# Linformer attention and a two-layer feed-forward network on one core: reciprocals of block 4 and q of batch 3 ahead of batch 3's projections in the queue

## The chip, the cores and the metric

The kernel runs on one core of a Trainium2 chip. The metric is the device time of one execution in microseconds (us); smaller is better. Before the change the median of three runs was 490.59 us.

A core has a matrix engine (TensorE, "PE" in the profile; its weight loads are "PEld"), a vector engine (VectorE, "DVE"), an engine for activation functions and copies (ScalarE, "ACT"), a general engine (GpSimd, "POOL") and a sync engine ("SP") that here only issues transfers. Each engine runs its own program in order. All transfers, from whatever engine they are issued, run on the core's 16 DMA engines. Those issued by GpSimd form the "software" queue of the profile (q0), those issued by sync the "hardware" queue (q1).

## The reference: what is computed

Linformer attention, then a feed-forward network with a sigmoid-approximated GELU:

```python
# q, k, v: (8 batches, 8 heads, 1024, 64); E, F: (64, 1024)
k_proj = np.einsum('ks,bhsd->bhkd', E, k)
v_proj = np.einsum('ks,bhsd->bhkd', F, v)
scale = 1.0 / np.sqrt(q.shape[-1])
scores = scale * np.matmul(q, k_proj.transpose(0, 1, 3, 2))
scores = scores - np.max(scores, axis=-1, keepdims=True)
attn = np.exp(scores)
attn = attn / (np.sum(attn, axis=-1, keepdims=True) + 1e-09)
attn_out = np.matmul(attn, v_proj)
# ... then with x = attn_out as (8192 tokens, 512):
h = x @ w_in                                  # (512, 2048)
g = h * (1.0 / (1.0 + np.exp(-1.702 * h)))
out = g @ w_out                               # (2048, 512)
```

## The kernel before

The 8192 tokens are worked off in 16 blocks of 512; batch b has blocks 2b and 2b+1. The heavy products of a block are those of the network (steps `u*.P*` for the first layer, `F*` for the second). The attention of later blocks is woven between them. The order of everything from block 2 on is written down as a list of words, `STEPS`; in round `j` a word `name+d` does the step `name` for block `j + d`. The words that this text speaks of:

- `pj`: the projections k' and v' of a batch, from the loaded k and v. `kb`: a cast of k' by VectorE. `kd`: a transposing transfer that makes `kt` of it. `vq`: copies of v'.
- `ld`: loads of k and v of the batch after. `hold`: a tiny GpSimd copy that reads `kt`, so that GpSimd's next load waits for `kt`.
- `qd`: a transposing transfer that makes `qT` of the loaded q of a batch, and, in the kernel before, right behind it in the program the loads of q of the batch after.
- `sc`: scores of a block, from `qT` and `kt`. `ex`: their exponentials. `su`, `den`: their sums. `ga`: a transfer that spreads the sums over 128 partitions (the gather). `rc`: the reciprocals, by VectorE. `sr`: a transfer that writes them to DRAM (`rdr`). `sb`: two transfers that read them back, spread over 64 partitions each (`rbc`, the broadcast).
- `va`: the unnormalised attention output. `mv`: its product with `rbc`, by VectorE, which gives the input `xT` of the network.

```python
        elif i == "va":
            eight([new(f"V{t}{e}", [P, TB]) for e in range(2)], [vqs[b % 2][:, 2 * t + e, :] for e in range(2)],
                  [expT[j][:, 2 * t + e, :] for e in range(2)])
        elif i == "mv":
            u = 2 * int(p[1]) + t
            nc.vector.tensor_tensor(x_of(j)[:, u, :], live[f"V{p[1]}{t}"], rbc[j][:, u, :], op=ALU.mult)   # L713
        # ...
        elif i == "ga":
            gather(j)()                                                   # sync: rc <- den (block 4: rc <- o_sb)
        elif i == "rc":
            nc.vector.reciprocal(rdens[j], rdens[j])                      # L728
        elif i == "sr":
            n = rdens[j].shape[1]
            rdr[j] = dram.tile([HP, 2, TB], F32, name="rdr")
            nc.sync.dma_start(out=rdr[j].rearrange("p e (r n) -> (p e r) n", n=n), in_=rdens.pop(j))   # L732
        elif i == "sb":
            rbc[j] = att.tile([P, HP, TB], F32, name="rbc", bufs=1)
            for e, r in enumerate((LO, HI)):
                nc.sync.dma_start(out=rbc[j][r], in_=rdr[j][None, :, e, :].to_broadcast([D, HP, TB]))  # L736
        elif i == "pj":
            kvps[b] = new("PJ", [P, H, D])
            proj(b)()
        elif i == "hold":
            nc.gpsimd.tensor_copy(held, kts[b % 2][:1, 0, :1])            # L741
        elif i == "ld" and b + 1 < B:
            load_kv(k, kt, b + 1, "k_sb")
            load_kv(v, vt, b + 1, "v_sb")
        # ...
        elif i == "kd":
            nc.sync.dma_start_transpose(out=kts[b % 2], in_=tmps["kb"].rearrange("k h d -> k (h d)"))  # L749
        # ...
        elif i == "qd":
            q_dma(b)()
            if b + 1 < B:
                load_q(b + 1)
```

The bank numbers that matter: `F1.0` goes into bank 0, which `va` (V01) uses too; `pj` goes into bank 1, which the products `u1.*` and `u3.*` use too (A1):

```python
    BANK = dict(FD=0, FB=4, FG=0, A0=6, A1=1, B0=7, B1=3, G0=2, G1=5, S10=5, S11=7, V00=4, V01=0,
                S00=3, S01=2, V10=6, V11=5, D0=2, D1=5, PJ=1)
```

Round 2 differs from the later ones: the attention of blocks 4 and 5 and the projections of batch 3 are put in at places of their own, by a table of words `name@block` that are done right after a named word of the list:

```python
    AHEAD = {
        (2, None): "... va.0@3:6,1 va.1@3:5,7 mv.0.0@3 ... su@4:0,3 den.0@4 den.1@4 ga@4 ",
        (2, "u1.c1+1"): "F7.1@2",
        (2, "gs4.0"): "pj@6:1 kb@6 kd@6 vq.0@6 vq.1@6 hold@6 ld@6",
        (2, "F4.1"): "rc@4 sr@4 sb@4 qd@6",
    }
```

Of the kernel before, what the change touches and what calls it, by code (L numbers as in the profile page):

```python
# [17 lines left out]
def kernel(ctx, tc, q, k, v, E, F,  # L18
                                                     moe_w_in, moe_w_out, out):
    nc = tc.nc  # L20
    B, H, S, D = q.shape
# [495 lines left out]
    def ffn2_parts(j, d, e, f, last):  # L517
# [73 lines left out]
        ex.1.1+3 xs.2+1 gs3.1 F2.0 F2.1 ex.1.0+3 xs.1+1 kd+4 ex.0.1+3 F6.0 F6.1 Fc2 u0.c1+1 su+3 u1.c1+1 gt+1  # L591
        u0.P6+1 den.0+3 u0.P2+1 Fo0 den.1+3 gs4.1 u1.P6+1 F7.0 u1.P2+1 u1.P5+1 u0.c2+1 F5.0 u1.c2+1 u0.g11+1
        u1.c3+1 F5.1 ga+3 Fc3 u1.P7+1 F7.1 u1.g11+1 xs.3+1 gs4.0 u1.P3+1 u2.P1+1 u0.P5+1 u1.d1+1 u3.P1+1 Fd1
        u0.c3+1 u1.P4+1 F4.0 u0.P7+1 sb+2 u1.d2+1 u0.d1+1 qd+4 u1.g21+1 u3.c1+1 F4.1 u1.g12+1 u3.P6+1 u3.c2+1
        u0.P4+1 u1.g22+1 u3.P5+1 u0.P3+1 u0.g21+1
    """.split()
    BANK = dict(FD=0, FB=4, FG=0, A0=6, A1=1, B0=7, B1=3, G0=2, G1=5, S10=5, S11=7, V00=4, V01=0,
                S00=3, S01=2, V10=6, V11=5, D0=2, D1=5, PJ=1)
# [5 lines left out]
    def step(name, j, banks=None):  # L604
# [7 lines left out]
        i, t = p[0], int(p[-1]) if p[-1].isdigit() else p[-1]  # L612
# [17 lines left out]
        if i[0] == "F" and i[1:].isdigit():  # L630
            i = int(i[1:])
            n = ("FD", "FB", "FG")[OF[i]]
            if i in (1, 5) and t == 0:
                new(n, [P, 2, MH])
            x, w = ffn2_ops(j)[i]
            for c in range(FH):
                nc.tensor.matmul(live[n][:, t], x[:, c, t * P:(t + 1) * P], w[:, c],  # L637
                                 start=(i in (1, 5) and t == 0 and c == 0),
                                 stop=(i in (2, 3, 4) and t == 1 and c == FH - 1), skip_group_check=True)
        elif i == "Fc1":  # L640
            copy(new("FB", [P, 2, MH]), live["FD"])
        elif i in ("Fc2", "Fc3"):
            tmps[i] = work.tile([P, 2, MH], F32, name="u1_sb" if i == "Fc2" else "u2_sb", bufs=1)
            copy(tmps[i], live["FB" if i == "Fc2" else "FG"])
        elif i == "Fo0":
            nc.scalar.copy(o(0)[:, :, :MH], live["FD"])
        elif i == "Fo1":
            nc.scalar.copy(o(1)[:, :, :MH], live["FB"])
        elif i == "Fd1":
            add(o(1)[:, :, MH:], live["FB"], tmps["Fc3"])  # L650
        elif i == "Fd2":
            add(o(0)[:, :, MH:], live["FG"], tmps["Fc2"])
        elif i[:2] == "st":
            g = int(i[2])
            ov = out[b * S:(b + 1) * S, :].rearrange("(p j) m -> p j m", j=J)[:, c * JB:(c + 1) * JB]
            nc.sync.dma_start(out=ov[:, 2 * g:2 * g + 2], in_=outs.pop((j, g)))
        elif i[0] == "u":
            n, m = int(i[1]), int(i[1]) % 2
            if not uu:
                uu.append(ldpool.tile([P, 4, 2, TH], F32, name="q_even"))  # L660
            gts[j] = gT
            u1, u2 = uu[0][:, m], uu[0][:, 2 + m]
            lo, hi = slice(2 * n, 2 * n + 2), slice(FH + 2 * n, FH + 2 * n + 2)
            if t[0] == "P":
                i = int(t[1])
                x = xT[j]
                a, w = {
                    1: (a11, x[:, KLO, TLO]), 2: (a12, x[:, KHI, TLO]), 3: (late[:, 3], x[:, KHI, THI]),
                    4: (a22, xw[:, 3]), 5: (late[:, 0], xw[:, 0]), 6: (late[:, 1], xw[:, 1]),
                    7: (late[:, 2], xw[:, 2])}[i]  # L670
                h = "ABG"[OF[i]] + str(m)
                if i in (1, 5):
                    new(h, [P, 2, TH])
                for r in range(2):
                    for c in range(KC // 2):
                        f = (2 * n + r) * P
                        nc.tensor.matmul(live[h][:, r], a[:, c, f:f + P], w[:, c],  # L677
                                         start=(i in (1, 5) and r == 0 and c == 0),
                                         stop=(i in (2, 3, 4) and r == 1 and c == KC // 2 - 1), skip_group_check=True)
            elif t == "c1":  # L680
                nc.scalar.copy(new(f"B{m}", [P, 2, TH]), live[f"A{m}"])  # L681
            elif t == "c2":
                copy(u1, live[f"B{m}"], f"c2.{n}")
            elif t == "c3":
                copy(u2, live[f"G{m}"], f"c3.{n}")
            elif t == "d1":
                add(u2, live[f"B{m}"], u2)
            elif t == "d2":
                add(u1, live[f"G{m}"], u1)
            else:  # L690
                out_, in_ = {"g11": (gT[:, lo, TLO], live[f"A{m}"]), "g21": (gT[:, hi, TLO], live[f"B{m}"]),
                             "g22": (gT[:, hi, THI], u2), "g12": (gT[:, lo, THI], u1)}[t]
                nc.scalar.activation(out_, in_, AF.Gelu_apprx_sigmoid)  # L693
        elif i[:2] == "gs":
            g_sum(j, int(i[2]), 4 * t, 4)
        elif i == "xs":
            x_sum(j, t)
        elif i == "sc":
            if j not in expT:
                expT[j] = att.tile([P, HP, TB], BF16, name="expT", bufs=3)  # L700
            eight([new(f"S{t}{e}", [P, TB]) for e in range(2)], [kts[b % 2][:, 2 * t + e, :] for e in range(2)],
                  [qT[b][:, c * JB:(c + 1) * JB, 2 * t + e, :] for e in range(2)])
        elif i == "ex":
            u = int(p[1])
            nc.scalar.activation(expT[j][:, 2 * u + t, :], live[f"S{u}{t}"], AF.Exp, scale=scale)
        elif i == "gt":
            gelu_table()
# [6 lines that stand above are left out]
        elif i == "su":  # L714
            d_ps = [new(f"D{e}", [P, TB]) for e in range(2)]
            for q_ in range(HP):
                for e in range(2):
                    r = HI if (q_ + e) % 2 else LO
                    nc.tensor.matmul(d_ps[e][32 * q_:32 * q_ + 32], ones[r, :32], expT[j][r, q_, :], start=True, stop=True)  # L719
        elif i == "den":  # L720
            if j not in rdens:
                pool, n = (work, "o1_sb") if j == 4 else (att, "den")
                rdens[j] = pool.tile([P, 2, TB], F32, name=n, bufs=1)
            nc.vector.tensor_copy(rdens[j][:, t, :], live[f"D{t}"])
        elif i == "ga":
            gather(j)()
# [18 lines that stand above are left out]
        elif i == "kb":  # L745
            tmps["kb"] = att.tile([KP, H, D], BF16, name="k_b")
            copy(tmps["kb"], kvps[b][LO])
        elif i == "kd":
            nc.sync.dma_start_transpose(out=kts[b % 2], in_=tmps["kb"].rearrange("k h d -> k (h d)"))  # L749
        elif i == "vq":  # L750
            r, xs_ = ((LO, X_LO), (HI, X_HI))[t]
            copy(vqs[b % 2][r].rearrange("k (u e) d -> k u e d", e=2),
                 kvps[b][HI].rearrange("k (u x) d -> k u x d", x=4)[:, :, xs_, :])
        elif i == "qd":
            q_dma(b)()
            if b + 1 < B:
                load_q(b + 1)
        elif i != "ld":
            raise KeyError(name)

    FIRST = {"u": 3, "gs": 3, "xs": 3, "gt": 3, "va": 4, "mv": 4, "sc": 6, "ex": 6, "su": 5, "den": 5, "ga": 5, "rc": 5,
             "sr": 5, "sb": 5}
    BATCH = ("qd", "pj", "kb", "kd", "vq", "ld")

    def due(name, j, now):

# [78 lines left out]
    for j in range(NBLK):  # L845
# [34 lines left out]
    }  # L880

    def ahead(j, after):
# [54 lines left out]
```

The softmax here doesn't subtract the row's maximum and nothing guards it: scores larger than these inputs give would overflow.

## Time and profile before

| what | value |
|---|---|
| time, median of 3 runs | 490.59 us (488.91 to 491.72) |
| span of the profiled execution | 487.4 us |
| mean granted TensorE clock in it | 0.989 |
| busy share: VectorE, ScalarE, GpSimd | 65%, 66%, 17% |
| software queue q0: packets, MB | 86816, 30.43 |
| hardware queue q1: packets, MB | 46020, 37.84 |

How to read the profile: "busy" is the time in which an engine works on an instruction. A page cuts the span into 40 equal slices and gives the busy share of each as one digit (9 is 90% or more); a row `PEclk` gives the clock that TensorE was granted, in tenths. A line of waits such as `A x L1 <- B y L2: 10.1, 1, 10.1` says that engine A, ahead of its instruction at line 1 that writes x, sat idle 10.1 us, once, until B's y was there. The chain of waits follows the program from its end back, at each step to what released the instruction. Lines of the timeline have start, length, engine, line, operation, names (written `out<-in`) and count; a `q` behind an engine's name is its sequencer, which for transfers shows the issue, not the transfer. "Landing" is when a transfer's completion is seen.

### The profile page before, as it was taken

The numbers are of one execution on the slowest core, as the hardware profiler recorded it, in microseconds if no ns is written. First come the engines' busy times: TensorE is split into PE (matmuls) and PEld (weight loads), VectorE is DVE, ScalarE is ACT, GpSimd is POOL, SyncE is SP. The second block draws the span as 40 slices with busy tenths as digits, with TensorE's granted clock in tenths as the row PEclk, the third lists the DMA queues.
The fourth block names the chain that finished last, engine by engine and source line by source line (L and its number), as shares of the span: only waits on it lengthen the run. The fifth ranks groups of instructions, "written<-read, shape, count | busy, mean of one in ns | idle before, by whom it ended". The sixth has DMA issues, their size and how long they took to land.

```text
span 487.4 us, 10497 instructions
## 1 busy us (share of the span) xinstructions
PE 467.6 (96%) x4331; PEld 358.0 (73%) x4331; DVE 316.3 (65%) x587; ACT 322.3 (66%) x559; POOL 83.2 (17%) x104
## 2 busy tenths in 40 slices
PE   8999999998919999999999999999999999999997
PEld 4644457456817878787887878787887878888886
DVE  4503785596607585866858585866758586858562
ACT  2665466474617686867879686867878695849472
POOL 7562160151105010410105010500000000000000
PEclk9999999999978999999999999999999999999999
DMA  9999999899599569992999369992191423412022
GB/s 169 200 189 208 220 176 176 190 208 143 90 221 208 99 144 209 210 142 89 161 235 131 89 153 211 214 128 89 31 201 40 89 89 89 146 31 87 0 87 87
DMA packets 132963, 69.19 MB, mean 142 GB/s; under 512 B 98340, under 2 KB 122420, under 8 KB 132916
## 3 DMA queue, kind: packets, MB, share of 16 engines
q0 software_dynamic: 86816, 30.43, 54.7%
q1 hardware_dynamic: 46020, 37.84, 31.1%
q8 instruction: 34, 0.56, 0.5%
q10 hardware_dynamic: 80, 0.26, 0.2%
q14 instruction: 13, 0.11, 0.1%
HBM read 72.88 MB, written 16.99 MB: 184 GB/s over the span
## 4 chain that ended last, share of the span: by engine, by line
PE 87%; DMA 5%; ACT 3%; DVE 2%; issue 1%; POOL 1%; SPq 0%; DVEq 0%; ACTq 0%; POOLq 0%
PE k_ps L637 32%; PE k_ps L677 31%; PE k_ps L426 9%; PE k_ps L533 4%; PE k_ps L273 3%; PE k_ps L438 3%; PE k_ps L183 3%; DMA rbc<-rdr 2%; DMA q_even<-in_q_dram 2%; DMA rdr<-rc 1%; ACT gT L693 1%; PE k_ps L719 1%; DVE xT L713 1%; POOL k_sb L58 0%; PE k_ps L398 0%
## 5 line engine op out<-in xcount | busy, mean ns | idle before, releaser
L623 DVE TENSOR_TENSOR q_even<-k_ps,q_even 128x512 f32<-128x512 f32 x104 | 70.5, 688 | 54.4 <-PE k_ps L677 53.3
L677 PE MATMUL k_ps<-xw,late 128*128 128x256 bf16 x624 | 89.5, 273 | 0.6 <-DVE xw L499 0.6
L677 PEld LDWEIGHTS <-late 128*128 128x128 bf16 x832 | 80.4, 98 | 12.8 <-PE k_ps L637 2.3
L637 PEld LDWEIGHTS <-sg 128*128 128x128 bf16 x832 | 81.2, 98 | 10.7 <-issue 1.4
L693 ACT ACTIVATE gT<-k_ps 128x512 bf16<-128x512 f32 x104 | 62.3, 600 | 25.7 <-PE k_ps L677 24.1
L637 PE MATMUL k_ps<-tw,sg 128*128 128x256 bf16 x624 | 76.8, 273 | 0.3 <-DVE u_sb L620 0.3
L637 PEld LDWEIGHTS <-gT 128*128 128x128 bf16 x624 | 61.8, 99 | 18.8 <-issue 10.7
L677 PEld LDWEIGHTS <-w_in_sb 128*128 128x128 bf16 x624 | 58.5, 98 | 17.6 <-issue 10.9
L693 ACT ACTIVATE gT<-q_even 128x512 bf16<-128x512 f32 x104 | 61.6, 631 | 10.8 <-DVE q_even L623 10.8
L620 ACT COPY q_even<-k_ps 128x512 f32<-128x512 f32 x65 | 37.0, 591 | 42.8 <-PE k_ps L677 42.8
L637 PE MATMUL k_ps<-w_out_sb,gT 128*128 128x256 bf16 x416 | 53.3, 278 | 10.3 <-DVE xT L713 10.1
L677 PE MATMUL k_ps<-xT,w_in_sb 128*128 128x256 bf16 x416 | 62.3, 274 | 0.1
L70 POOL DMA_DIRECT2D q_sb<-in_q_dram x48 | 42.1, 905 | 114.3 <-DMA qT<-q_sb 89.2
L426 PE MATMUL k_ps<-xT,w_in_sb 128*128 128x512 bf16 (+1 forms) x200 | 42.7, 371 | 0.0
L507 DVE TENSOR_TENSOR sg<-gT 128x1024 bf16<-128x1024 bf16 (+2 forms) x64 | 41.4, 648 | 1.9 <-ACT gT L693 1.5
L428 ACT ACTIVATE gT<-k_ps 128x512 bf16<-128x512 f32 (+1 forms) x50 | 28.9, 580 | 18.0 <-PE k_ps L426 17.7
L713 DVE TENSOR_TENSOR xT<-k_ps,rbc 128x512 bf16<-128x512 f32 x52 | 33.4, 679 | 11.3 <-DMA rbc<-rdr 11.3
L426 PEld LDWEIGHTS <-w_in_sb 128*128 128x128 bf16 x200 | 19.3, 98 | 21.3 <-issue 0.8
L677 PE MATMUL k_ps<-xw,w_in_sb 128*128 128x256 bf16 x208 | 31.8, 276 | 0.0
L677 PE MATMUL k_ps<-xT,late 128*128 128x256 bf16 x208 | 31.2, 273 | 0.0
L681 ACT COPY k_ps<-k_ps 128x512 f32<-128x512 f32 x52 | 29.2, 587 | 2.7 <-DVE xT L713 1.2
L620 DVE COPY q_even<-k_ps 128x512 f32<-128x512 f32 x39 | 25.6, 683 | 8.1 <-PE k_ps L677 8.1
(136 smaller groups left out, 563.5 us busy)
## 6 DMA issues: line engine op xcount, KB each, us to landing
out_dram<-o_sb SPq DMA_DIRECT2D x31, 512.0 KB
rbc<-rdr SPq DMA_DIRECT2D x24, 512.0 KB
k_sb<-in_k_dram POOLq DMA_DIRECT2D x7, 1024.0 KB, 9.8
v_sb<-in_v_dram POOLq DMA_DIRECT2D x7, 1024.0 KB, 15.7
q_sb<-in_q_dram POOLq DMA_DIRECT2D x48, 128.0 KB, 6.2
w_in_sb<-in_moe_w_in_dram POOLq DMA_DIRECT2D x8, 256.0 KB, 10.3
w_out_sb<-in_moe_w_out_dram POOLq DMA_DIRECT2D x4, 512.0 KB, 11.5
q_even<-in_q_dram POOLq DMA_DIRECT2D x12, 128.0 KB, 12.9
```

Source lines behind the costliest of these rows:

```text
L70: nc.gpsimd.dma_start(out=qt[b][:, j], in_=qv[:, j])
L426: nc.tensor.matmul(h_ps, w_in_sb[:, kc, fc * P:(fc + 1) * P], xT[j][:, kc, ts], start=(kc == 0), stop=(kc == KC - 1))
L428: nc.scalar.activation(gts[j][:, fc, ts], h_ps, AF.Gelu_apprx_sigmoid)
L507: nc.vector.tensor_tensor(t[i - 1], in0, in1, op=ALU.add if i == 1 else ALU.subtract)
L533: nc.tensor.matmul(dst, a[:, k, tc_ * P:(tc_ + 1) * P], w[:, k], start=(first and (one or tc_ == 0) and k == 0), stop=(final and k == FH - 1),
L620: (nc.scalar.copy if n in ON_ACT else nc.vector.tensor_copy)(out_, in_)
L623: nc.vector.tensor_tensor(out_, in0, in1, op=ALU.add)
L637: nc.tensor.matmul(live[n][:, t], x[:, c, t * P:(t + 1) * P], w[:, c], start=(i in (1, 5) and t == 0 and c == 0), stop=(i in (2, 3, 4) and ...
L677: nc.tensor.matmul(live[h][:, r], a[:, c, f:f + P], w[:, c], start=(i in (1, 5) and r == 0 and c == 0), stop=(i in (2, 3, 4) and r == 1 an ...
L681: nc.scalar.copy(new(f"B{m}", [P, 2, TH]), live[f"A{m}"])
L693: nc.scalar.activation(out_, in_, AF.Gelu_apprx_sigmoid)
L713: nc.vector.tensor_tensor(x_of(j)[:, u, :], live[f"V{p[1]}{t}"], rbc[j][:, u, :], op=ALU.mult)
```

## The change

Two groups of words of round 2 become one, at one place: behind `u2.P1+1`, which lies two words behind `gs4.0` (where the projections stood) and ahead of `F4.1` (where the reciprocals stood). In the new group the reciprocals of block 4, their write and broadcast and the transpose of q of batch 3 come ahead of the projections of batch 3. The loads of q of the batch after are taken out of `qd` into a word of their own, `lq`, so that they can stand elsewhere than behind `qd`: in round 2 they are the last of the group, behind the k and v loads of batch 4, which still wait for `kt`. In the later rounds `lq` follows `qd` at once. No computation is added or left out.

What it is for: on the sync queue the write and the broadcast of the reciprocals are issued ahead of the transposes of q and k', and ahead of batch 4's loads on GpSimd's queue, rather than behind those loads.

```diff
@@ STEPS @@
-        u0.c3+1 u1.P4+1 F4.0 u0.P7+1 sb+2 u1.d2+1 u0.d1+1 qd+4 u1.g21+1 u3.c1+1 F4.1 u1.g12+1 u3.P6+1 u3.c2+1
-        u0.P4+1 u1.g22+1 u3.P5+1 u0.P3+1 u0.g21+1
+        u0.c3+1 u1.P4+1 F4.0 u0.P7+1 sb+2 u1.d2+1 u0.d1+1 qd+4 lq+4 u1.g21+1 u3.c1+1 F4.1 u1.g12+1 u3.P6+1
+        u3.c2+1 u0.P4+1 u1.g22+1 u3.P5+1 u0.P3+1 u0.g21+1
@@ step @@
         elif i == "qd":
             q_dma(b)()
-            if b + 1 < B:
-                load_q(b + 1)
-        elif i != "ld":
+        elif i == "lq" and b + 1 < B:
+            load_q(b + 1)
+        elif i not in ("ld", "lq"):
             raise KeyError(name)
@@ AHEAD @@
-        (2, "gs4.0"): "pj@6:1 kb@6 kd@6 vq.0@6 vq.1@6 hold@6 ld@6",
-        (2, "F4.1"): "rc@4 sr@4 sb@4 qd@6",
+        (2, "u2.P1+1"): "rc@4 sr@4 sb@4 qd@6 pj@6:1 kb@6 kd@6 vq.0@6 vq.1@6 hold@6 ld@6 lq@6",
```

The words between the two places, in the list:

```python
# gs4.0 u1.P3+1 u2.P1+1 u0.P5+1 u1.d1+1 u3.P1+1 Fd1 u0.c3+1 u1.P4+1 F4.0 u0.P7+1 ... F4.1
```

More of the change, by code (lines that the diff above doesn't have):

```diff
@@ L762 @@
              "sr": 5, "sb": 5}
-    BATCH = ("qd", "pj", "kb", "kd", "vq", "ld")
+    BATCH = ("qd", "pj", "kb", "kd", "vq", "ld", "lq")
     def due(name, j, now):
```

## The prediction

> **What bounds the kernel now.** I read the engine totals first, then the slices, then the waits of the one slice that stands out, then the chain through it, then the queues that feed it. By the totals TensorE is busy 467.6 us, 96% of the span, VectorE 65%, ScalarE 66%. Two rows of the 40 slices (12.2 us each):
>
> ```profile
> PE   8999999998919999999999999999999999999997
> ...
> PEclk9999999999978999999999999999999999999999
> ```
>
> TensorE is full nearly everywhere, so an instruction that it is spared, or a wait that it is spared, moves the end one to one. There is one hole: the slice with the 1 (134 to 146 us), followed by slices with a lower granted clock. After it every slice is 9 until the last. The waits between 112 and 160 us (engine, line waited for, total us, times, longest):
>
> ```profile
> DVE xT L713 <- DMA rbc<-rdr: 11.3, 1, 11.3
> ...
> PE k_ps L637 <- DVE xT L713: 10.1, 1, 10.1
> ```
>
> VectorE's normalisation of block 4 (`mv`, L713) waits for rbc, the broadcast reciprocals; TensorE waits for VectorE because the next product F1.0 goes into the bank that `mv` has to read first. The chain of waits through the hole (start, us, what):
>
> ```profile
> 127.72 6.43 DMA rdr<-rc
> ...
> 134.96 10.10 DMA rbc<-rdr
> ```
>
> The reciprocal (0.27) ends right ahead of the first line, and `mv` starts at 145.19, 0.1 us after the last. So 17 us of transfers (16 KB out, then 2 x 512 KB back) stand between the reciprocal and `mv`. Why so slow? The sync queue, and GpSimd's, in order of time:
>
> ```profile
> 114.51 0.57 SPq L322 DMA_DIRECT2D rc<-o_sb  x1
> 116.71 0.52 SPq L322 DMA_DIRECT2D rc<-den  x1
> 123.49 1.18 SPq L749 DMA_TRANSPOSE kt<-k_b  x1
> 127.72 0.34 SPq L732 DMA_DIRECT2D rdr<-rc  x1
> 134.23 1.34 SPq L736 DMA_DIRECT2D rbc<-rdr  x2
> 135.89 10.57 SPq L263 DMA_TRANSPOSE qT<-q_sb  x1
> ```
>
> ```profile
> 126.31 0.87 POOL L58 DMA_DIRECT2D k_sb<-in_k_dram  x1 [0.31 <-issue]
> 127.17 0.88 POOL L58 DMA_DIRECT2D v_sb<-in_v_dram  x1
> ```
>
> The k and v loads of batch 4 went out 1.4 and 0.6 us ahead of the 16 KB write, and everything after them crawls. Before they went out the engines had nothing to do. DMA from 118 to 128 us, in slices of 0.25 us:
>
> ```profile
> GB/s 154 155 164 157 145 109 93 62 28 30 33 13 0 0 0 0 0 0 0 0 0 0 0 33 0 0 36 165 61 1 0 0 0 0 0 0 0 0 0 29
> ```
>
> The gather of block 4 (`rc<-o_sb`, issued 114.51; `rc<-den` is that of block 5) sat among the q loads of batch 3. In the single packets, its 128 pieces are read by 119.6, those of block 5 by 121.0, where this row falls to 0. So the sums of block 4 lie there at about 120, and until 127.7 the row shows next to nothing but the small kt transpose: the reciprocals could have been taken and sent.
>
> [...] 16 KB took 6.43 us behind the loads, and 1.7 us from issue to landing for the rdr write that GpSimd issued at 94.04. [...] in the single DMA packets no rbc packet appears until about 4 us after its issue at 134.23, then both queues run. [...] The trace has exactly one such drop: granted clock 0.50 from 142 to 150 us, 0.88 from 150 to 152, 1.00 from 152.
>
> **The change, part by part.** No arithmetic is added or removed; words move in the step list.
>
> 1. *Reciprocal, write, broadcast of block 4 go first.* The gather has landed at about 120. VectorE is idle from 118.2 to 122.8, so the reciprocal (343 ns, median of 12) fits: done about 120.4, without pushing back the cast of k' at 122.77. The write then meets the last q packets and after them empty engines: I take 1.7 to 2.5 us instead of 6.4, landed near 122.5. The two broadcasts landed 5.1 to 7.0 us after issue where GpSimd issued them at 96.3; the second goes out at 123.3, so rbc is there at 128.4 to 130.3. In the odd stage shown below `mv` starts 0.7 us after `va.0`, so it wants rbc at 133.8. Slack 3 to 5 us: the stall goes.
>
> 2. *What the stall costs.* I measure from `va.0` to the first scores of the batch ahead (`sc.0`) in this stage, and in the next odd stage without a stall:
>
> ```profile
> 133.12 0.41 PE L273 MATMUL k_ps<-expT,vq 64*32 64x512 bf16 x8
> ...
> 150.85 0.62 PE L273 MATMUL k_ps<-qT,kt 64*32 64x512 bf16 x16
> ...
> 200.34 0.41 PE L273 MATMUL k_ps<-expT,vq 64*32 64x512 bf16 x8
> ...
> 205.60 0.63 PE L273 MATMUL k_ps<-qT,kt 64*32 64x512 bf16 x16
> ```
>
> 17.73 against 5.26: 12.47 us too much. The wait is 10.1 of it. The 24 products from its end to `sc.0` took 4.92 us (145.93 to 150.85) against 2.71 for the same 24 in the other stage (202.89 to 205.60): 2.2 us for the half clock. With no wait there is no clock drop, so both go.
>
> 3. *Projections of batch 3 two products later.* `pj` follows u1.P3 and u2.P1 (0.43 us each) rather than preceding them. In the trace it starts at 120.82, held 0.7 us by the activation that frees its bank, and the product that reuses the bank, u3.P1, starts at 124.29 just after the copies out of it. That chain (activation, pj 1.9, cast 0.7, two copies 0.75) is unchanged; the two products fill its gap in front and leave one behind. Gain 0, give or take 0.3.
>
> 4. *q's transpose ahead of k's on the sync queue.* qd goes out at about 124. It landed (GpSimd's next q load was released) at 149.4, 4.3 us after rbc; in later batches some 5.8 us after the last rbc packet. So qT is there at 133 to 136. The sync queue itself is held for the 9 to 11 us of the issue, which ended 2.9 us before landing, so kd (k') goes out at 130 to 133.5 instead of 123.5 and lands 2.3 us later or just behind qT: 133.5 to 136.5. `sc.0` of block 6 needs both at 133.12 + 5.26 = 138.4. Slack about 2 to 5 us, one of the two thinnest in the plan. The 1 MB of stores of block 2 follow on the same queue, done near 139, and their buffer is written again only at 156.6 - 12.5 = 144.
>
> 5. *Loads of batch 4 behind kt.* `held` is released at 134 to 137 instead of 125.8; k, v and then q go out in one run. In batch 3 that pattern, k issued at 97.6, had its last q packet at 121: 23.4 us. From 136 that makes 159.4 for q; k and v, 17.2 us from v's issue to landing here, are there by about 154. `pj` of batch 4 comes at 174.1 - 12.5 = 161.7 and its q transpose at 175.7. Hidden.
>
> Sum: -12.5 + 0 + a possible short wait at `sc.0`, mean +0.3: 490.59 - 12.2 = 478.4. All later slices are full of TensorE work, so nothing downstream absorbs it.
>
> **Rivals.** *The wait moves to kt and qT.* For it: qd took 13.5 us from issue to landing in the kernel before; from 124 or 125 that gives 137.5 to 138.5, and kt behind it up to 140. Against it: that time included waiting for an rbc transfer slowed by the loads. It would cost up to 2 us[...]: about 479.5. *The collision moves on to block 5.* Its broadcast goes out at 158.2 - 12.5 = 145.8, into the k, v, q loads of batch 4 that formerly were half done by then. With the 10.8 us of the bad case it lands at 156.6; its `mv` comes at 172.8 - 12.5 = 160.3. For it: 128-byte q packets keep the engines busiest of all. Against it: 3.7 us of slack [...]. If it bites, 2 to 5 us are lost: 480.5 to 483.5. *The reciprocal is not early*, because the gather lands later than 122 and VectorE, in order, then holds up the cast of k' and with it bank 1: a shift of some tenths per us of lateness, and rbc at 133 or later: 479 to 482. *The stall was hiding load time*, TensorE then running into late k and v at `pj` of batch 4: it would need them over 7 us later than I reckon; unlikely.
>
> **Range and chances.** The mechanism is direct and every slack positive, so the middle lies near the full 12.5 us. The low end is the full gain with a second below it for the spread of the runs before (488.91 to 491.72); the high end leaves 3 us for one of the first two rivals. Two per cent is 9.8 us; to miss it a rival must cost 2.7 us. I give 0.82 to faster, 0.17 to within 2%, 0.01 to slower.
>
> **What would show it.** Right: no digit below 9 in TensorE's row from 134 us on and no dip in its clock row; the rdr write issued near 120.5, rbc near 122.7, qT near 124, kt after 130; from `va.0` to `sc.0` some 5.3 us; k, v loads near 136. Wrong: a wait of TensorE at the scores L273 released by qT or kt (rival one), of L713 by rbc at block 5 (rival two), or a reciprocal after 122.8 (rival three). The prediction fails altogether if L713 still waits several us for rbc at block 4, which would mean that the loads were not what slowed it.

## Result: 2.7% faster, and the profile after

The changed kernel takes 476.94 us (median of 4 runs, 476.44 to 477.87) against 490.14 us (488.91 to 491.72, 4 runs): ratio 0.9731, 95% interval 0.9698 to 0.9764. Two later comparisons on other occasions gave 0.9755 (0.9734 to 0.9777) and 0.9738 (0.9721 to 0.9754), that is 12.1 and 12.6 us. The prediction was 478.4 us, 476.4 to 481.6, and faster.

TensorE's row and its clock row on the page of the kernel after (40 slices, now 11.9 us each):

```profile
PE   8999999998999999999999999999999999999997
...
PEclk9999999999999999999999999999999999999999
```

The hole is gone and so is the dip in the clock (mean granted clock 1.000, 0.989 before). The sync queue of the kernel after, in order of time (start, length of the issue):

```profile
120.36 0.34 SPq L732 DMA_DIRECT2D rdr<-rc  x1
122.95 1.34 SPq L736 DMA_DIRECT2D rbc<-rdr  x2
124.64 8.90 SPq L263 DMA_TRANSPOSE qT<-q_sb  x1
133.64 1.19 SPq L749 DMA_TRANSPOSE kt<-k_b  x1
134.93 0.99 SPq L656 DMA_DIRECT2D out_dram<-o_sb  x2
135.98 0.79 SPq L732 DMA_DIRECT2D rdr<-rc  x1
```

The write is followed by the broadcast 2.6 us later (6.5 before). GpSimd's `held` copy and the first load of batch 4, and the products that the broadcast used to hold up, from GpSimd's and TensorE's timelines:

```profile
136.06 0.18 POOL L741 COPY held<-kt 1x1 bf16<-1x1 bf16 x1 [20.68 <-DMA kt<-k_b]
136.54 0.87 POOL L58 DMA_DIRECT2D k_sb<-in_k_dram  x1 [0.31 <-issue]
```

```profile
132.81 0.41 PE L273 MATMUL k_ps<-expT,vq 64*32 64x512 bf16 x8
...
138.07 0.62 PE L273 MATMUL k_ps<-qT,kt 64*32 64x512 bf16 x16
```

From `va.0` to `sc.0` are 5.26 us, with no wait, against 17.73 before. The loads start 10 us later than before (136.54 against 126.31), and TensorE has no wait for them.

The opening of the program varies by some three microseconds between the profiled executions, before any of this begins (the gather of block 4 goes out between 114.11 and 117.27 us). So I also compare from the issue of the gather of block 4 (`rc<-o_sb`) to the end of the span: 487.4 - 114.51 = 372.9 us before, 474.7 - 114.11 = 360.6 after, a difference of 12.3.

### The profile page after: what moved, and what is told of

It is laid out like the page before. It is cut to its first block, busy times and chain, and to the rows that moved or that the text cites. A ratio compares the mean times of both kernels' runs of the same rounds, so it can differ in the third digit from the quotient of the medians.

```text
span 474.7 us, 10486 instructions
## 1 busy us (share of the span) xinstructions
PE 463.9 (98%) x4323; PEld 356.2 (75%) x4331; DVE 316.6 (67%) x587; ACT 322.1 (68%) x559; POOL 83.2 (18%) x104
## 4 chain that ended last, share of the span: by engine, by line
PE 91%; DMA 3%; ACT 3%; DVE 2%; POOL 1%; issue 1%; DVEq 0%; ACTq 0%; POOLq 0%
PE k_ps L677 34%; PE k_ps L637 33%; PE k_ps L426 9%; PE k_ps L533 5%; PE k_ps L273 3%; PE k_ps L438 3%; PE k_ps L183 3%; DMA v_sb<-in_v_dram 3%; ACT gT L693 1%; PE k_ps L719 1%; DVE xT L713 1%; POOL k_sb L58 0%; POOL v_sb L58 0%; PE k_ps L398 0%; PE k_ps L413 0%
## 5 line engine op out<-in xcount | busy, mean ns | idle before, releaser
L677 PEld LDWEIGHTS <-late 128*128 128x128 bf16 x832 | 80.4, 98 | 12.8 <-PE k_ps L637 2.3
L637 PE MATMUL k_ps<-w_out_sb,gT 128*128 128x256 bf16 x416 | 51.6, 273 | 0.1
L713 DVE TENSOR_TENSOR xT<-k_ps,rbc 128x512 bf16<-128x512 f32 x52 | 33.5, 680 | 0.0
## 6 DMA issues: line engine op xcount, KB each, us to landing
q_even<-in_q_dram POOLq DMA_DIRECT2D x12, 128.0 KB, 13.2
```

Of the source, the lines that this page charges most:

```text
L677: nc.tensor.matmul(live[h][:, r], a[:, c, f:f + P], w[:, c], start=(i in (1, 5) and r == 0 and c == 0), stop=(i in (2, 3, 4) and r == 1 an ...
```

## Experiments

The theory: the loads of batch 4 on the DMA engines slowed the write and broadcast of the reciprocals (10 us of wait), and the half clock (0.50) after the wait cost 2.2 us more. The first rival: the reciprocals were simply taken too late, whatever else was on the engines. The second: which of the change's other parts (q's transpose, the place of `pj`, the order of q's loads) are needed. The first experiment changes the kernel before; the diffs of all others are against the changed kernel.

### The clock apart from the wait

In the kernel before, 44 products of zeros that nobody reads, where TensorE waits. They are added work; all of the kernel's own work stays.

```diff
             ahead(j, word)
+            if (j, word) == (3, "va.1+1"):
+                d_ps = bank(1, [P, TB])
+                for _ in range(44):
+                    nc.tensor.matmul(d_ps, zeros[:, :P], zeros, start=True, stop=True)
```

> The kernel before, with 44 products of zeros (128x128 by 128x512, some 0.216 us each, 9.5 us in all) put on TensorE into a bank that nobody reads, at the place where it waits for block 4's mv. The wait stays, but TensorE is busy in it. Theory (2.2 us of the 12.5 are the half clock, a cost apart from the wait): no dip in the clock row, the products from the end of the wait to the scores take about 2.7 us instead of 4.92, and the time falls by 2.2 us to about 488. Rival (the slow stretch after the wait has another cause, for instance VectorE catching up): the stretch stays near 4.9 us and the time within 0.5 us of the kernel before.

Measured: 488.14 us against 490.38, ratio 0.9958 (0.9936 to 0.9981). TensorE's first product after the wait in the kernel before, then its timeline here:

```profile
145.93 1.86 PE L637 MATMUL k_ps<-w_out_sb,gT 128*128 128x256 bf16 x8 [10.11 <-DVE xT L713]
```

```profile
136.55 9.67 PE L907 MATMUL k_ps<-zeros 128*128 128x512 bf16 x44
...
147.45 1.03 PE L637 MATMUL k_ps<-w_out_sb,gT 128*128 128x256 bf16 x8 [0.80 <-DVE xT L713]
...
150.48 0.62 PE L273 MATMUL k_ps<-qT,kt 64*32 64x512 bf16 x16
```

The wait is as long as it was (`va.0` at 134.45, so 13.0 us to the first product after it, 12.8 in the kernel before), but that group of eight products takes 1.03 us instead of 1.86 and the stretch to the scores 3.03 us instead of 4.92; the rival falls. So some 2 us of the 12.5 are the clock alone. That is shown, since nothing else was changed: adding 9.7 us of useless work made the kernel faster.

### Only the loads later

The words stay at their old places; GpSimd reads `qT` of batch 3 before it issues the loads of batch 4.

```diff
-        (2, "u2.P1+1"): "rc@4 sr@4 sb@4 qd@6 pj@6:1 kb@6 kd@6 vq.0@6 vq.1@6 hold@6 ld@6 lq@6",
+        (2, "gs4.0"): "pj@6:1 kb@6 kd@6 vq.0@6 vq.1@6",
+        (2, "F4.1"): "rc@4 sr@4 sb@4 qd@6 holdq@6 ld@6 lq@6",
...
+        elif i == "holdq":
+            nc.gpsimd.tensor_copy(held, qT[b][:1, 0, 0, :1])
```

> The words stay where they were before the change (projections behind gs4.0, reciprocals, write, broadcast and q's transpose behind F4.1); only the loads of batch 4 wait, for the transposed q of batch 3, that is behind the broadcast. Theory (the loads on the DMA engines made the wait; the place of the words is what lets the rest of it go): write landed about 2.3 us after its issue at 127.4 instead of 6.4, broadcast 6 to 7 us after its own, rbc near 136.5, so TensorE waits 2 to 3 us for mv, without a clock dip; qT then lands near 141.5 and the scores may wait about another us. Time 479.5 to 481.5. Rival (the reciprocals are simply taken too late; loads matter little): TensorE still waits 7 us or more, time 486 or higher.

Measured: 482.99 us against 490.38, ratio 0.9849 (0.9824 to 0.9873). The chain of waits (start, us, what), and TensorE's wait for `mv`:

```profile
127.71 2.75 DMA rdr<-rc
...
131.27 6.63 DMA rbc<-rdr
```

```profile
PE k_ps L637 <- DVE xT L713: 3.0, 1, 3.0
```

The reciprocals are taken as late as before (127.71 against 127.72), but the two transfers take 9.4 us instead of 16.5. TensorE's wait for `mv` is 3.0 us instead of 10.1. So the loads made 7 of the 10 us of wait; the first rival accounts for the last 3.

The single packets show where the 7 us went. In the kernel before, the write had its first packet 4.2 us after its issue and the broadcast 4.0 us after; here it is 0.8 and 1.5. That is 5.9 of the 7.1 us by which the two transfers are shorter. Once it ran, the broadcast took 6.0 us from its first to its last packet before, 5.2 here. So the loads made the two transfers start late far more than they made them run slowly. The same holds for the whole kernel before: of its twelve broadcasts on the sync queue, the four issued while k and v loads were moving had their first packet 2.9 to 4.0 us later, the other eight 1.4 to 1.5 us later. Why a transfer starts late behind such loads the runs do not show.

The total came out above the expectation, because I had ruled out a clock dip after a wait of 2 to 3 us; that was an estimate of mine, which no trace had shown. There was one (windows: span, then busy time of TensorE, its loads, VectorE, ScalarE, GpSimd, clock, DMA share, GB/s):

```profile
136.00:138.00 2.00, 0.00 (x0) 0.00 (x0) 0.00 (x0) 0.00 (x0) 0.00 (x0) 0.96 1.22 174
138.00:139.00 1.00, 0.23 (x2) 0.17 (x2) 0.98 (x2) 0.00 (x0) 0.00 (x0) 0.50 1.27 290
```

A mean of 0.96 over the first 2 us, at a clock of 0.50 once it drops, means that it dropped at about 137.8: 2.0 us after TensorE's last product ended at 135.8. From the end of the wait to the scores took 5.2 us, 2.5 more than at full clock.

### The group early, but the loads not held back

```diff
-        (2, "u2.P1+1"): "rc@4 sr@4 sb@4 qd@6 pj@6:1 kb@6 kd@6 vq.0@6 vq.1@6 hold@6 ld@6 lq@6",
+        (2, "u2.P1+1"): "rc@4 sr@4 sb@4 qd@6 pj@6:1 kb@6 kd@6 vq.0@6 vq.1@6 ld@6 lq@6",
```

> The changed kernel without the tiny copy that makes GpSimd wait for kt: the k and v loads of batch 4 go out right behind v' products, near 122.5, at about the same time as the broadcast. Everything else is as in the changed kernel. Theory (a broadcast that shares the engines with 2 MB of loads takes about 10 us, and the transposes queue behind it): rbc near 133 to 134.5, so mv waits 0 to 1 us; qT near 139 to 141 and kt behind it, so TensorE waits 1 to 4 us at the scores of block 6 (due at 138.1); time 478 to 481. Rival (once the write is early, the order against the loads no longer matters): time within 0.7 us of the changed kernel's 476.9.

Measured: 488.46 us against 490.38, ratio 0.9959 (0.9943 to 0.9975). Both expectations missed: all but 2 us of the gain are gone, where I had reckoned with 478 to 481 us and the rival with 477. TensorE's longest wait between 100 and 180 us, and the sync queue:

```profile
PE k_ps L273 <- DMA kt<-k_b: 8.0, 1, 8.0
```

```profile
123.17 1.34 SPq L736 DMA_DIRECT2D rbc<-rdr  x2
124.87 19.52 SPq L263 DMA_TRANSPOSE qT<-q_sb  x1
144.49 1.19 SPq L749 DMA_TRANSPOSE kt<-k_b  x1
```

The broadcast was in time but for 0.3 us (that wait of VectorE at L713), as I had thought. What collapsed is the transpose of q: its issue held the queue for 19.5 us instead of 8.9, and k's transpose stood behind it. TensorE waited for kt instead of rbc, and had the clock dip on top. The single DMA packets, counted by the microsecond in which they start (a count of mine from the trace):

```
us          loads of batch 4 (1024 B)    transposes (256 B)
            no hold      changed         no hold    changed
131            98           0                14       1122
134            86           0                79       1134
137           153           0               155          0
139           156          60               152          0
141           155         179               151          0
143            31         174               477          0
144             0         154              1094          0
```

From 135 us on, when the broadcast is through, the transposes beside the loads advance at the pace of the loads, one packet for one; without loads they reach 1134 per us, seven times that. q's transpose has 4096 packets, the loads have 2048 in all, so at one for one it can't end before the loads do. The broadcast, 512 packets of 2048 bytes, took 9.1 us from its first to its last packet in this run and 5.4 in the changed kernel. What this sharing does to a transpose I had not seen in the prediction.

### Is it the transposes' order, or the sharing?

As the last one, but k's transpose ahead of q's.

```diff
-        (2, "u2.P1+1"): "rc@4 sr@4 sb@4 qd@6 pj@6:1 kb@6 kd@6 vq.0@6 vq.1@6 hold@6 ld@6 lq@6",
+        (2, "u2.P1+1"): "rc@4 sr@4 sb@4 pj@6:1 kb@6 kd@6 vq.0@6 vq.1@6 ld@6",
+        (2, "F4.1"): "qd@6 lq@6",
```

> The changed kernel without the hold and with the transpose of q behind F4.1, so behind k's on the sync queue. In the run without the hold TensorE waited 8.0 us at the scores for kt, which stood behind q's transpose in the queue. Theory ([...] the 4096 packets of 256 bytes of q's transpose advance no faster than the 1 KB packets of the loads, some 150 per us each, until the loads are done near 142.5): kt is early now, near 134, but qT lands near 145 to 146, so TensorE waits 6 to 8 us at the scores all the same, now for qT; time 486 to 488.5. Rival (it was only that kt stood behind qT in the queue): no wait above 2 us at the scores, time below 480.

Measured: 487.39 us against 490.41, ratio 0.9948 (0.9932 to 0.9963). TensorE's waits and q's transpose on the sync queue:

```profile
PE k_ps L273 <- DMA qT<-q_sb: 5.4, 1, 5.4
PE k_ps L637 <- DVE xT L713: 1.5, 1, 1.5
```

```profile
127.67 16.52 SPq L263 DMA_TRANSPOSE qT<-q_sb  x1
```

The wait is now for qT itself; the rival falls. It is 5.4 us rather than the 6 to 8 expected, because TensorE had already lost 1.5 us to a late broadcast, which I had not expected: issued at 124.16, with the loads just ahead of it, it had its first packet 4.3 us later. So it is the sharing of the engines with the loads that must be avoided. The next run differs from this one in nothing but the `hold`.

### q's transpose last, loads held back

```diff
-        (2, "u2.P1+1"): "rc@4 sr@4 sb@4 qd@6 pj@6:1 kb@6 kd@6 vq.0@6 vq.1@6 hold@6 ld@6 lq@6",
+        (2, "u2.P1+1"): "rc@4 sr@4 sb@4 pj@6:1 kb@6 kd@6 vq.0@6 vq.1@6 hold@6 ld@6",
+        (2, "F4.1"): "qd@6 lq@6",
```

> The changed kernel, but the transpose of q of batch 3 goes back behind F4.1, so on the sync queue it comes behind k's transpose, and the loads of batch 4 go out before it. Theory ([...] kt now lands soon after rbc, near 130.5, the loads go out near 131, and the transpose of q runs partly among them): qT lands between 135 and 139, against 138.1 wanted; TensorE waits 0 to 1.5 us at the scores of block 6; time 476.5 to 478.5. Rival (q ahead of the projections is needed as much as the reciprocals): a wait of 3 us or more at the scores, time 480 or higher.

Measured: 478.28 us against 490.38, ratio 0.975 (0.9719 to 0.9782). TensorE's timeline at `va.0` and `sc.0`:

```profile
135.97 0.41 PE L273 MATMUL k_ps<-expT,vq 64*32 64x512 bf16 x8
...
141.23 0.63 PE L273 MATMUL k_ps<-qT,kt 64*32 64x512 bf16 x16
```

These are 5.26 us, with no wait; from the gather to the end 478.0 - 117.27 = 360.7 us, as in the changed kernel (360.6). q ahead of the projections is thus not needed: kt stands behind the broadcast in the queue, so `held` was released at 134.08 only, 7.9 us after the broadcast's issue at 126.21, the loads' first packets came at 138.3, and by then q's transpose was through to its last packets. The loads are held back either way, and the rival falls. Against the last run, which lacks only the `hold` copy, this is 9.1 us: the little copy, which existed before, earns 9.1 of the 12.1 us, once kt stands behind the broadcast in the queue.

### q's loads ahead of k's and v's again

```diff
-        (2, "u2.P1+1"): "rc@4 sr@4 sb@4 qd@6 pj@6:1 kb@6 kd@6 vq.0@6 vq.1@6 hold@6 ld@6 lq@6",
+        (2, "u2.P1+1"): "rc@4 sr@4 sb@4 qd@6 lq@6 pj@6:1 kb@6 kd@6 vq.0@6 vq.1@6 hold@6 ld@6",
```

> The changed kernel with the q loads of batch 4 ahead of its k and v loads again (right behind q's transpose in the program). GpSimd then waits for qT (near 134.5), issues eight q loads (0.88 us each, to near 142), and only then k and v. Theory (q has 14 us of slack and k, v about 6): v lands near 160, just about when the projections of batch 4 want it (161.4): 0 to 2 us slower than the changed kernel. Rival (the order of these loads is immaterial): within 0.3 us; or the broadcast of block 5, issued near 145.5, gets through earlier or later and moves mv of block 5 (due 160), which would show as a wait of L713 there.

Measured: 480.36 us; the changed kernel on the same occasion 478.03 (ratios 0.9815, 0.9792 to 0.9838, and 0.9755, 0.9734 to 0.9777). TensorE at the projections of batch 4:

```profile
165.32 0.38 PE L183 MATMUL k_ps<-v_sb,eft 128*64 128x512 bf16 x1 [1.85 <-DMA v_sb<-in_v_dram]
```

v comes 1.9 us late, so the rival falls. From the gather to the end are 478.6 - 115.82 = 362.8 us, 2.3 more than in the changed kernel beside it (360.5, below). So "q loaded last" is worth 2.3 us, a little over the 0 to 2 expected. The need for it follows from delaying the loads: with k and v behind q there is no slack left.

### The place of the projections

The whole group two words earlier, behind gs4.0:

```diff
-        (2, "u2.P1+1"): "rc@4 sr@4 ...
+        (2, "gs4.0"): "rc@4 sr@4 ...
```

> The changed kernel with the whole group at the old place of the projections (behind gs4.0, two TensorE words earlier). Theory (step 3 of the prediction: the chain activation, projections, casts on bank 1 sets u3.P1's start, whatever fills the gaps; moving pj is worth nothing): the same as the changed kernel within 0.4 us, u3.P1 at about 124.0 as there. Rival (pj's later place gave the half us by which the gain beat the 12.5): 0.4 to 1 us slower.

The changed kernel itself, on the same occasion:

> The changed kernel once more, beside the next three on the same chip, so that differences of some tenths can be read: 476.9 within 0.6 us.

Measured: 477.76 us (0.9753, 0.9735 to 0.9771) and 478.03. From the gather to the end 475.7 - 115.20 = 360.5 us here, 474.8 - 114.29 = 360.5 there. No difference, as step 3 said.

### A version that beats both

Step 3 also says what would help: the projections not in bank 1.

```diff
-        (2, "u2.P1+1"): "rc@4 sr@4 sb@4 qd@6 pj@6:1 kb@6 kd@6 vq.0@6 vq.1@6 hold@6 ld@6 lq@6",
+        (2, "gs4.0"): "rc@4 sr@4 sb@4 qd@6 pj@6:6 kb@6 kd@6 vq.0@6 vq.1@6 hold@6 ld@6 lq@6",
+        (2, "u1.P3+1"): "u0.P5@3 u1.d1@3 u3.P1@3",
```

> An attempt at a version that beats both: the group behind gs4.0 with the projections in bank 6 (free since 116.8) instead of bank 1, so that they need not wait for the activation of u1, and u0.P5, u1.d1, u3.P1 of round 2 ahead of u2.P1, which now is the one that needs the projections' bank back. Theory: TensorE's idle time of 1.0 us plus 0.2 to 0.7 around the projections shrinks to 0.3 or less; time 0.7 to 1.3 us below the changed kernel, about 476. Rival (VectorE and ScalarE, which get the same work in another order, hand the time back in the next products): no difference beyond 0.3 us.

> The version with the projections in bank 6 once more, beside the changed kernel on the same chip. Theory: 0.9 us below the changed kernel, as the trace showed from the gather of block 4 to the end (359.6 against 360.5 us); rival: a difference below 0.4 us.

> The changed kernel, as the other side of that comparison: 477 to 478 us.

Measured: 476.86 and 476.36 us, against 478.03 and 477.85 for the changed kernel beside it; against the kernel before 0.9728 (0.9711 to 0.9745) and 0.9708 (0.969 to 0.9726). The product that has to wait for the copies out of the projections' bank, first in the changed kernel, then here:

```profile
123.99 0.60 PE L677 MATMUL k_ps<-xT,w_in_sb 128*128 128x256 bf16 x4 [1.04 <-ACT vq L620]
```

```profile
124.36 0.60 PE L677 MATMUL k_ps<-xT,w_in_sb 128*128 128x256 bf16 x4 [0.17 <-ACT vq L620]
```

0.87 us of idle time fewer, and from the gather to the end 475.0 - 115.36 = 359.6 us against 360.5: the gain reaches the end. The second pair gives 474.3 - 114.59 = 359.7 against 476.3 - 115.77 = 360.5. The medians differ by 1.2 and 1.5 us, the intervals overlap slightly, so the size is better taken from the traces: 0.8 to 0.9 us. The bank and the order of three words were changed together; what each gives alone is not shown.

## Why the prediction was right

- **Bound and hole.** TensorE decides: 12.5 us less between `va.0` and `sc.0` (17.73 to 5.26) are 12.3 us less from the gather to the end, in the two profiled executions. The medians of the three comparisons differ by 13.2, 12.1 and 12.6 us, where 12.2 was predicted.
- **Step 1.** The write was expected near 120.5 and issued at 120.36, the broadcast near 122.7 and at 122.95; `mv` started at 133.53, 0.7 us after `va.0`, without a wait. The reciprocal ran at 119.98, so the rival of a late gather didn't come true. Why it works is shown from two sides: the loads late alone take 7 of the 10 us of wait, the reciprocals early alone, without the hold, move the wait to the transposes (8.0 us). "Everything after them crawls" was the right sign but a rough picture: most of the loss was a late start of the two transfers.
- **Step 2.** The half clock was put at 2.2 us; the run with a busy wait saved 2.2 us in its time and 1.9 us in the stretch itself.
- **Step 3.** u3.P1 starts 9.88 us after the gather's issue (123.99 - 114.11), before 9.78. Moving the group by two words changed nothing.
- **Step 4.** qT went out at 124.64 (about 124 said), kt at 133.64 (130 to 133.5 said), `held` saw it at 136.06; 2.0 us of slack to the scores at 138.07, at the low end of the 2 to 5 given. The rival that the wait moves to kt and qT didn't come true here, but it is the true danger: without the hold it cost 8 us and the clock. My argument against it, that its 13.5 us came from the slow broadcast ahead of it, holds for the kernel before: there the transpose's packets ran from 143.1 to 148.0, when the loads were through. What it lacked is that the transpose of q beside the loads drops to a seventh of its packet rate (151 to 156 per us, 1134 without them).
- **Step 5.** The loads went out at 136.54 (136 said); GpSimd's wait for v ended at 155.6 (about 154), with no wait of TensorE for k or v, so the rival that the stall hid load time fell too; the projections of batch 4 came at 161.36 (161.7). q's last packet came at 167.6 rather than 159.4, still 7.8 us ahead of q's transpose at 175.4. The rival of block 5: its broadcast went out at 145.46 and, among the loads, its last packet came near 157, against 156.6 reckoned and `mv` of block 5 at 159.98. Slack under 3 us, no wait. What the rival said of the 128-byte q packets the kernel before shows: the packet times of q0 added up to 224.7% of the 16 engines' span from 112 to 118 us, among q loads, and to 122.0% from 130 to 138, among those of k and v with 1024 bytes.

No step failed. What the prediction lacked is that step 5's delay of the loads is no side effect: with the same group of words and the loads not held back, all but 1.9 us of the gain were gone.

## What to carry to other kernels

When a wait is for a small transfer, look at what went out just ahead of it on any queue, and move the bulk load behind the chain that is waited for; moving the chain forward alone may only hand the wait to the next transfer in the same queue (8.0 us here, for kt). Count packets, not bytes: q's transpose, 4096 packets of 256 bytes, was held here to the packet rate of the load beside it (151 to 156 per us, against 1134 without it). And when loads are delayed, order them by who needs them first; here that was worth 2.3 us of 12.5.

## What the runs showed of the hardware

- In the run without the hold, GpSimd's loads with packets of 1024 bytes and sync's transpose with packets of 256 bytes advanced one for one, 151 to 156 packets per us each at 137, 139 and 141 us; with no load beside them the 256-byte packets of the changed kernel ran at 1134 per us at 134 us. Both queues run on the same 16 DMA engines by the page's account: in the kernel before q0 took 54.7% of their span, q1 31.1%.
- A broadcast issued on the sync queue while k and v loads were moving had its first packet 2.9 to 4.0 us after its issue, otherwise 1.4 to 1.5 us after (kernel before, four and eight of them).
- A wait of 3.0 us was enough for the half clock (0.50) in the run with only the loads later, where it came 2.0 us after TensorE's last product; in the kernel before it came 4.4 us after (the last product ended at 135.8, the mean of 0.56 from 140 to 142 us puts the drop at 140.2). The half clock lasted 10.24 us in the kernel before and 6.83 us in that run. A wait of 1.50 us in the run with k's transpose first brought no drop: the eight products after it took 1.03 us, as in the run with the busy wait. What sets the moment of the drop no run shows.
- Keeping TensorE busy with 44 products of zeros (9.7 us) through the wait for `mv` in the kernel before was worth 2.2 us of the 490 (490.38 to 488.14).
